# A gelu moved in ScalarE's order, thirteen split matmuls and new offsets of the 320-column operands, in a gated spectral mixer with a GeGLU branch

## The chip, the cores and the metric

The kernel runs on one core of one Trainium2 chip. The metric is the time of one execution on the device in microseconds (us); the median of several executions is compared.

## The reference, cut to what matters

```python
def _A_ref(x, w1, b1, w2, b2):
    z = rfft2(x, axes=(1, 2)).reshape(B, H, Wf, 4, 160)          # x is (2, 1, 4096, 640)
    hr = relu(zr @ w1[0] - zi @ w1[1] + b1[0]); hi = relu(zi @ w1[0] + zr @ w1[1] + b1[1])
    or_ = hr @ w2[0] - hi @ w2[1] + b2[0];      oi_ = hi @ w2[0] + hr @ w2[1] + b2[1]
    # both shrunk towards zero by 0.01
    return irfft2(or_ + 1j * oi_)
def _B_ref(x, w_gate, w_up, w_down):
    return (gelu(x @ w_gate) * (x @ w_up)) @ w_down              # 640 -> 1728 -> 640
g = sigmoid((x * gate_w).sum(-1, keepdims=True))
return g * _A_ref(...) + (1 - g) * _B_ref(...)
```

The relu, the blocks of 160 columns and the tanh form of gelu are written short here.

## The kernel before, in words

Every product is made of float32r operands in a high and a low part: a weight (wh, wl) and a moving operand (xh, xl) give three matmuls wh xh, wh xl and wl xh into one PSUM bank (`prod`, `run`, `mm3`). ScalarE makes the high part (`high`, L283), VectorE or GpSimd the low part (`low`, L286). The work has three stages, all of them on one core and issued in an order written out by hand.

**Stage 1, to about 1405 us: gate and up products.** The 8192 tokens are taken 512 at a time in 48 token groups (`keys`, counted by `i`): three rounds over the sixteen groups of tokens, with four, four and six pairs of weight tiles `t`. One group runs `quad` for each of its pairs, j = 0, 1, 2, ... (the first group runs `plain`). `quad` is Strassen's scheme with seven products instead of eight (g1, s3, s2, g2, s1, s4, u2), each a `run` of six or nine matmuls of 256 columns into half a bank. It is in two parts: the first four products are made at once, the last three (half5, half3, half4) are kept in `Q` and made in between the next quad's products. So the order of TensorE around the change is: half5 of the old quad (s1 into its bank X), g1 of the new quad into a new X, s3 into C, half3 of the old quad (s4 into the old X), s2 into the new X on top of g1, half4 of the old quad (u2), g2 into A.

Each bank must be read before TensorE goes on in it. ScalarE copies X after g1 (tile p, `copy`, L492), after s2 (u2) and after s1 (u4); a matmul that goes on in X waits for that copy. VectorE adds A to p1 (L516, L534 and the like for the others), ScalarE takes the gelu of p1 in place (`gelu`, L493), later the gelu of X after s4 into h, and VectorE multiplies (L536, L537). In the kernel before, the gelu of p1 stands in half5, right behind the copy of u4 and so ahead of the new quad's copy of p.

Between the products stand seven hooks per quad (`hook(0)` to `hook(6)`). They run what `spread` put into `slots`: splits of the next group's tokens (`x_prep`), preparation of weights (`w_prep`, `wd_pre`), and the 64 steps of the first transform (`a_load`, `a_split`, `a_gate`, `a_step`; `steps_a` names the group and the place of each). Each engine takes its instructions in the order in which they are issued; loads and stores of the SP queue too.

**Stage 2, to about 1842 us: the spectral branch.** Sixteen chunks of frequencies, each with four steps (64 in all, S = 64; the order of the last ones is shuffled). A chunk needs four tiles sc (`sc_load`, L746), a product `rest` whose result zz is stored to DRAM, and `zl_load`, which reads it back in another layout (L777, L779). `lead` says how many steps earlier than the others the last chunk does that. `main_z` (matmuls of 128 columns in plain float32, f and sc, L754), `mlp1`, `mlp2` (320 columns, wm with h, wl with hl), `y_split` (tile ys) and `inv1` (ys with i1) follow. `fin` lists what of the last stage is loaded in which step: `wl(part, j, ...)` loads the down weights wx that were prepared in stage 1 (`wd_load`, L1054).

**Stage 3: down projection and last transform.** 32 rounds of `down`, each of 144 matmuls of 320 columns, tile wx moving and tile ho as weights (L469), with `inv2` in between (s2s moving, v as weights, twelve matmuls).

**Where the tiles start.** Tiles come from pools: small (2560 bytes per partition each), big (5376), still (1024), mid (4096), tiny (1024). As the program lays them out, big, still and small tiles start at a multiple of 256 bytes, and mid tiles 192 bytes past one, because of the unused tile "gap" of 192 bytes. `off` shifts a view inside its tile by so many words of 4 bytes. 320 columns are 1280 bytes, five times 256, so all operands of a tile keep its place modulo 256.

Of the kernel before, what the change touches and what calls it, by code (L numbers as in the profile page):

```python
# [11 lines left out]
F32R = mybir.dt.float32r  # L12
# [200 lines left out]
def spectral_mix_kernel(ctx: ExitStack, tc: tile.TileContext, a):  # L213
# [29 lines left out]
    def big(shape, dt=F32, name="big", off=0):  # L243
        return view(pool[1].tile([P, 1344], dt, name=name, tag="big", bufs=17), shape, off)
# [4 lines left out]
    def mid(shape, dt=F32, name="mid", off=0):  # L249
        return view(pool[4].tile([P, 1024], dt, name=name, tag="mid", bufs=13), shape, off)  # L250
# [209 lines left out]
    def prod(ws, x):  # L460

        ops = []
        for (wh, wl), (xh, xl) in zip(ws, x):
            ops += [(wh, xh), (wh, xl), (wl, xh)]
        return ops

    def run(dst, ops, first=True):
        for i, (l, r) in enumerate(ops):
            nc.tensor.matmul(dst, l, r, start=first and i == 0, stop=i == len(ops) - 1, skip_group_check=True)  # L469
# [14 lines left out]

    Q = []

    def quad(key, t, hook):

        o, w = XO[key], WG[t]
        half = lambda: bank()[:, :256]  # L490
        T = lambda n: tiny([P, 256], name=n)
        copy = lambda d, s_: nc.scalar.activation(d, s_, AF.Copy)  # L492
        gelu = lambda d, s_: nc.scalar.activation(d, s_, AF.Gelu_apprx_tanh)  # L493
        old = Q.pop() if Q else [lambda: None] * 3

        old[0]()
        hook(0)
        X = half()
        run(X, prod(w["g1"], x_of(o, "b11", ("k4", 0))))
        p1 = T("p1")  # L500
        copy(p1, X)
        hook(1)
        C = half()
        run(C, prod(w["s3"], x_of(o, "t3", ("k4", 1))))
        hook(2)
        old[1]()
        hook(3)
        run(X, prod(w["s2"], x_of(o, "t2", "t5")), first=False)
        u2 = T("u2")
        copy(u2, X)  # L510
        hook(4)
        old[2]()
        hook(5)
        A = half()
        run(A, prod(w["g2"], x_of(o, "b21")))
        nc.vector.tensor_add(p1, A, p1)  # L516
        hook(6)
        v = {}

        def half5():  # L520
            run(X, prod(w["s1"], x_of(o, "t1", "t5")), first=False)
            u4 = v["u4"] = T("u4")
            copy(u4, X)
            gelu(p1, p1)
            nc.vector.tensor_add(u4, C, u4)

        def half3():
            run(X, prod(w["s4"], x_of(o, "b22")), first=False)
            h = v["h"] = small([P, 512], name="h")
            gelu(h[:, 256:], X)  # L530

        def half4():
            run(C, prod(w["u2"], x_of(o, "t4")), first=False)
            nc.vector.tensor_add(u2, C, u2)  # L534
            h = v["h"]
            nc.vector.tensor_mul(h[:, 256:], h[:, 256:], v["u4"])  # L536
            nc.vector.tensor_mul(h[:, :256], u2, p1)  # L537
            h_store(key[1], t, h)
        Q.append([half5, half3, half4])
# [406 lines left out]
    def y_split(b, c, pb):  # L946
        for j in range(2):
            y = Y.pop((b, c, pb, j))
            t = YS[b, c, pb, j] = big([P, 2, 2, 320], F32R, name="ys")
            split(t[:, 0], t[:, 1], y.rearrange("p r n o -> p r (n o)"),  # L950
                  nc.gpsimd if j == 1 and (b, c, pb) < (1, NCH - 2, 1) else nc.vector)

# [94 lines left out]
    def wd_load(j, part):  # L1047
        d = WM.setdefault(j, {})
        kinds = {(5, 2): ((big, 4), (small, 2)), (6, 1): ((small, 2),) * 2, (6, 2): ((small, 2),) * 3}.get(
            (j, part), (((big, 4),) if part < 2 else ((mid, 3),) * 2))  # L1050
        at_, parts = 4 * part, []

        def go(t, k, n):
            ld(t.rearrange("p h d -> p (h d)").bitcast(F32), dr(wdf[j], 320 * k, [[14 * 320, P], [1, 320 * n]]))  # L1054
        for i, (kind, n) in enumerate(kinds):
            off = {} if kind is small else {"off": 16} if kind is mid else {"off": 63 if j > 4 else 0}
            t = kind([P, n, 320], F32R, name="wx", **off)
            if part < 2 or i == 0:
                go(t, at_, n)
            else:  # L1060
                later.append(lambda t=t, k=at_, n=n: go(t, k, n))
            parts += [t[:, k] for k in range(n)]
            at_ += n
        for k in range(len(parts) // 2):
            d[FORMS[2 * part + k]] = parts[2 * k], parts[2 * k + 1]
# [7 lines left out]
            S2[i].append(raw)  # L1073

    def c_split(i):
        m = [mid([P, 3, 320], F32R, name="s2s", off=15) for k in range(3)]
        raws, S2[i] = S2[i], {}
        for k in (0, 2, 1, 3):
            h, l = (m[(2 * k + e) // 3][:, (2 * k + e) % 3] for e in range(2))
            split(h, l, raws[k // 2][:, 320 * (k % 2):320 * (k % 2) + 320])  # L1080
            S2[i][k] = h, l
# [34 lines left out]
        d["s4"] = d.pop("s2")  # L1116

    def h_op(i, name, eng=nc.vector):
        t = big([P, 5, 2, P], F32R, name="ho", off=1)
        uh, ul = (still([P, 2, P], F32R, name="ho") for k in range(2))  # L1120
        src, six = HR[i].pop(name) if name in ("s1", "s3", "s4", "a22") else HR[i][name]
        split(t[:, :, 0], t[:, :, 1], src, eng)
        if name == "a22":
            high(uh[:, 0], six[:, 0])
            high(ul[:64, 1], six[:64, 1])
            high(uh[64:, 1], six[:64, 1])
            low(ul[:, 0], six[:, 0], uh[:, 0], eng)
            low(uh[:64, 1], six[:64, 1], ul[:64, 1], eng)
        elif name in HALF:
            high(uh, six)  # L1130
            low(ul[:, 0], six[:, 0], uh[:, 0], eng)
            low(uh[64:, 1], six[:64, 1], uh[:64, 1], eng)
        else:
            high(uh, six)
            low(ul, six, uh, eng)
        HO[i, name] = [(t[:, j, 0], t[:, j, 1]) for j in range(5)] + [(uh[:, j], ul[:, j]) for j in range(2)]
# [92 lines left out]
    at(46, 2, gates, 1)  # L1229

    def i1_load():
        I1.append(big([P, 5, 2, P], F32R, name="i1", off=1))
        nc.gpsimd.dma_start(I1[0], a["i1"])
    last = len(keys) - 1
    at(last - 1, 1, i1_load)
# [32 lines left out]
    def spread(i, s, fs):  # L1268

        for k, f in enumerate(fs):  # L1270
# [1 line left out]
            while j < last and q >= points(j):  # L1272
                j, q = j + 1, q - points(j)
            slots.setdefault((j, q), []).append(f)
    steps_a = [(i, j) for i in (*range(2, 16, 3), *range(17, 31), *range(33, 46)) for j in range(1 if i < 17 else 2 if i < 33 else 3)][:64]

    def back(i, s, f):
        if s < 0:
# [38 lines left out]
    for i, key in enumerate(keys):  # L1317
        gr, tp = key
        nxt = keys[i + 1] if i < last else None
        quads = [t for t in groups[gr] if t < NPAIR]  # L1320
        nq = len(quads)
        if nxt:
            if not i:
                x_raw(nxt)
            z = 7 * (nq - 1)
            for k, s in enumerate((5, 8, 11, 14, 16, 18, z + 1, z + 4, z + 6) if gr < 2 else
                                  (6, 9, 13, 17, 21, z + 1, z + 2, z + 3, z + 3, z + 5)):
                if k < 9 or nxt[0] == 2:
                    f0, f1, f2_ = x_prep(nxt, k)
                    spread(i, s - 1, [f0])  # L1330
                    spread(i, s + 1, [f1, f2_])
            if gr < 2 and nxt[0] == 2:
                spread(i, z + 7, x_prep(nxt, 9))
        for j, t in enumerate(quads):
            def hook(k):
                for f in slots.get((i, 7 * j + k), ()):
                    f()
            (quad if i else plain)(key, t, hook)
            if gr == 2 and j == 1:
                mixed(key)  # L1340
            if i % 16 == 15:
                WG.pop(t)
            if 0 < i + 1 < last and j == nq - 1:
                x_raw(keys[i + 2])
            n = len(late)
            for f, *args in todo.get((i, j), []):
                f(*args)
            new = late[n:]
            del late[n:]
            flush()  # L1350
            late.extend(new)
        for q in range(7 * nq, 7 * nq + 14) if i == last else ():
            for f in slots.get((i, q), ()):
                f()
        XO.pop(key)
# [9 lines left out]
    todo = {}  # L1365
    for ch in range(1, 2 * NCH):
        b, c = chunks[ch]
        lead = 1 if ch == 2 * NCH - 1 else 0
        if ch > 1:
            at(4 * ch - 4 - lead, 0, sc_load, b, c)  # L1370
        at(4 * ch - 3 - lead, 1, rest, b, c)
        at(4 * ch - 2 - lead, 1, zl_load, b, c)
# [7 lines left out]
    def events(i, j):  # L1380
        for f, *args in todo.get((i, j), []):
# [3 lines left out]
           S - 13: wl(0, 1),  # L1385
           S - 12: [*wl(2, 6), (wd_later,)],
           S - 11: [*wl(2, 0), (wd_later,)],
           S - 10: wl(1, 6),
           S - 8: [(v_load, 0), *wl(2, 1), (wd_later,)],
           S - 6: wl(0, 2),  # L1390
           S - 5: wl(0, 3, 4, 5),
# [91 lines left out]
```

## Time and profile before

| | |
|---|---|
| median of 3 runs | 2579.09 us (2576.34 to 2587.95) |
| the profiled execution's own time | 2581.51 us |
| its span, first to last instruction | 2579.8 us |
| mean granted clock of TensorE | 0.997 |
| TensorE busy | 2555.5 us (99%), 20340 matmuls |
| VectorE, ScalarE, GpSimd busy | 2020.8 us (78%), 1504.9 us (58%), 381.4 us (15%) |

How to read it: PE is TensorE's matmuls, PEld its weight loads, DVE is VectorE, ACT ScalarE, POOL GpSimd, SP the queue that issues most DMAs. A row of a group has the line, the engine, the operation, what is written and read, the shapes and the count, then busy time in us and the mean duration of one in ns, then the idle time ahead of them and what ended most of it. Matmuls overlap: one lasts about 0.28 us (256 columns) or 0.31 us (320 columns) from its start to its end, while the next starts much sooner. In a timeline row stand the start, the length of the merged instructions, the engine and the line, and in brackets how long the engine was idle before and for what. A row of the waits has who waited for whom, the total in us, how often and the longest.

### The profile page before, as it was taken

Reading aid. Unit: us, or ns where it says so; the run is one execution under the profiler, and the core shown is the slowest. Engines: PE = TensorE matmul, PEld = TensorE weight load, DVE = VectorE, ACT = ScalarE, POOL = GpSimd, SP = SyncE. Lnnn points to the kernel's source line nnn. Section 1 sums busy time; section 2 is a strip of 40 time slices with the busy share of each in tenths; the row PEclk is TensorE's granted clock in tenths of the full one; section 3 lists DMA queues with packets and bytes.
Section 4 is the critical chain, followed back from the end, with each engine's and each line's share of the span. In section 5 each row is a group of like instructions: output and inputs, shape, how many; then the busy total and the mean of one; then the engine's idle time right before and its main releaser. Section 6 shows DMA issues by size and latency. Waiting matters only on the chain.

```text
span 2579.8 us, 54180 instructions
## 1 busy us (share of the span) xinstructions
PE 2555.5 (99%) x20340; PEld 2548.2 (99%) x20340; DVE 2020.8 (78%) x4179; ACT 1504.9 (58%) x3540; POOL 381.4 (15%) x382
## 2 busy tenths in 40 slices
PE   9999999999999999999999999999999999999999
PEld 9999999999999999999999999999999999999999
DVE  7767677777778777787547886887899899889997
ACT  5555555666665566666445886787644444444443
POOL 0000000000000000000002111111233333333332
PEclk9999999999999999999999998999999999999999
DMA  6555556676676677777566543547844443444432
GB/s 226 184 195 195 186 192 224 216 228 219 210 226 220 202 225 235 241 243 228 186 217 189 156 144 121 166 142 244 287 152 149 154 153 134 134 149 154 154 134 92
DMA packets 337562, 483.81 MB, mean 188 GB/s; under 512 B 25676, under 2 KB 207948, under 8 KB 337300
## 3 DMA queue, kind: packets, MB, share of 16 engines
q1 hardware_dynamic: 321748, 438.80, 52.6%
q0 software_dynamic: 15552, 41.56, 4.8%
q8 instruction: 160, 2.62, 0.4%
q14 instruction: 102, 0.84, 0.1%
HBM read 300.62 MB, written 179.64 MB: 186 GB/s over the span
## 4 chain that ended last, share of the span: by engine, by line
PE 95%; DMA 2%; DVE 2%; ACT 1%; issue 0%; SPq 0%; DVEq 0%; ACTq 0%
PE bank L469 76%; PE bank L302 13%; PE bank L754 3%; PE bank L613 1%; PE bank L810 1%; PE bank L811 1%; DMA zl<-zl 0%; DMA xraw<-in_xT_dram 0%; DMA zl<-zz 0%; PE bank L813 0%; DMA wx<-wdf 0%; DMA sc<-scr 0%; ACT xs L283 0%; DVE wl L710 0%; DVE as L615 0%
## 5 line engine op out<-in xcount | busy, mean ns | idle before, releaser
L469 PE MATMUL bank<-xo,w 128*128 128x256 f32 x11736 | 1371.7, 278 | 15.2 <-ACT p L492 7.8
L469 PEld LDWEIGHTS bank<-xo,w 128*128 128x128 f32 x11736 | 1359.5, 188 | 19.7 <-ACT p L492 10.5
L469 PE MATMUL bank<-wx,ho 128*128 128x320 f32 x4608 | 682.5, 309 | 0.0
L469 PEld LDWEIGHTS bank<-wx,ho 128*128 128x128 f32 x4608 | 678.5, 188 | 0.0
L492 ACT ACTIVATE u<-bank 128x256 f32<-128x256 f32 x408 | 156.6, 384 | 291.2 <-PE bank L469 287.3
L283 ACT ACTIVATE ho<-hraw 128x640 fp32r<-128x640 f32 (+3 forms) x384 | 179.4, 518 | 150.0 <-PE bank L469 149.2
L286 DVE TENSOR_TENSOR ho<-hraw,ho 128x640 fp32r<-128x640 f32 (+3 forms) x384 | 241.6, 678 | 4.1 <-ACT ho L283 3.1
L534 DVE TENSOR_TENSOR u<-bank,u 128x256 f32<-128x256 f32 x204 | 86.4, 423 | 134.8 <-PE bank L469 131.6
L286 DVE TENSOR_TENSOR xs<-xr,xs 64x640 fp32r<-64x640 f32 x128 | 105.0, 820 | 77.6 <-ACT xs L283 71.8
L286 DVE TENSOR_TENSOR xo<-xraw,xo 128x512 fp32r<-128x512 f32 x209 | 143.1, 685 | 21.3 <-ACT xo L283 19.7
L615 DVE TENSOR_TENSOR as<-bank,as 64x320 f32<-64x320 f32 x256 | 113.8, 483 | 28.3 <-ACT as L614 27.2
L283 ACT ACTIVATE xo<-xraw 128x512 fp32r<-128x512 f32 x209 | 129.2, 626 | 5.4 <-DMA xraw<-in_xT_dram 4.4
L302 PE MATMUL bank<-wm,h 128*128 128x320 f32 x768 | 131.6, 305 | 0.0
L493 ACT ACTIVATE h<-bank 128x256 f32<-128x256 f32 x204 | 78.0, 382 | 91.8 <-PE bank L469 88.0
L493 ACT ACTIVATE p<-p 128x256 f32<-128x256 f32 x204 | 84.5, 414 | 60.1 <-DVE p L516 59.4
L1097 POOL TENSOR_TENSOR hraw<-hraw 128x640 f32<-128x640 f32 x64 | 87.4, 1381 | 217.7 <-DMA hraw<-hD 132.8
L302 PEld LDWEIGHTS bank<-wm,h 128*128 128x128 f32 x768 | 114.5, 187 | 0.1
L286 DVE TENSOR_TENSOR s2s<-s,s2s 128x320 fp32r<-128x320 f32 x128 | 113.4, 943 | 0.5 <-ACT s2s L283 0.5
L566 POOL MEMSET h<- 64x512 f32 x16 | 8.4, 522 | 707.8 <-PE bank L469 338.1
L283 ACT ACTIVATE ho<-hs 128x640 fp32r<-128x640 f32 (+1 forms) x128 | 67.1, 572 | 70.4 <-PE bank L469 65.5
L1160 ACT ACTIVATE uu<-bank,gs 128x320 f32<-128x320 f32 x120 | 54.3, 525 | 89.4 <-PE bank L302 89.4
L614 ACT ACTIVATE as<-bank 64x320 f32<-64x320 f32 x256 | 96.8, 427 | 15.6 <-PE bank L613 12.8
(168 smaller groups left out, 3507.8 us busy)
## 6 DMA issues: line engine op xcount, KB each, us to landing
xo<-xD SPq DMA_DIRECT2D x124, 512.0 KB
xraw<-in_xT_dram SPq DMA_DIRECT2D x225, 256.0 KB
hD<-h SPq DMA_DIRECT2D x224, 256.0 KB
hraw<-hD SPq DMA_DIRECT2D x128, 320.0 KB
xD<-xo POOLq DMA_DIRECT2D x64, 512.0 KB, 4.2
xr<-in_x_dram SPq DMA_DIRECT2D x64, 320.0 KB
scr<-as SPq DMA_DIRECT2D x64, 320.0 KB
sc<-scr SPq DMA_DIRECT2D x64, 320.0 KB
```

Source lines behind the costliest of these rows:

```text
L283: nc.scalar.activation(dst, src, AF.Copy, scale=scale)
L286: eng.tensor_sub(dst, src, hi.bitcast(F32))
L302: nc.tensor.matmul(dst, l, r, start=i == 0, stop=i == len(ops) - 1)
L469: nc.tensor.matmul(dst, l, r, start=first and i == 0, stop=i == len(ops) - 1, skip_group_check=True)
L492: copy = lambda d, s_: nc.scalar.activation(d, s_, AF.Copy)
L493: gelu = lambda d, s_: nc.scalar.activation(d, s_, AF.Gelu_apprx_tanh)
L534: nc.vector.tensor_add(u2, C, u2)
L614: nc.scalar.activation(stg[hi, cs], pa[lo, :320], AF.Copy)
L615: nc.vector.tensor_add(stg[hi, cs], pa[hi, :320], stg[hi, cs])
L754: nc.tensor.matmul(pz[:, kp * P:(kp + 1) * P], SC[b, c, kp][:, o:o + P], ft, start=True, stop=True)
L1097: eng.tensor_sub(d["a21"][k], d["a11"][k], d["a21"][k])
L1160: nc.scalar.activation(uu[n2][:, cs], pe[:, :320], AF.Copy, scale=gs[:, b, 0, n2:n2 + 1])
```

## The change

It does six things.

- In `quad` the gelu of p1 moves from half5 to the head of half3. On ScalarE it then comes behind the new quad's copy of p and behind what hooks 0, 1 and 2 issue, ahead of the gelu of h.
- `quad` gets an argument `fresh`. Where it holds, the last matmul of the product g2 is written as two matmuls of 128 columns with the same weights. It holds for the second pair (j = 1) of the token groups 1, 2, 5, 9, 13, ... 45, thirteen times in all.
- The offsets: ys goes from the start of its big tile to 15 words; wx from 0 or 63 words (big) and 16 (mid) to 15 and 31; s2s (mid) from 15 to 31; ho and i1 (big) from 1 word to 0. In bytes modulo 256: ys and most wx from 0 to 60, the wx of the pairs 5 and 6 in big tiles from 252 to 60, s2s from 252 to 60, ho and i1 from 4 to 0. wx in small tiles stay at 0, v stays at 0.
- The list of the 64 steps of the first transform has none in token group 14 any more; all later ones move on by one place.
- The last chunk of stage 2 has its loads and its `rest` two steps ahead instead of one.
- The two loads of wx for pair 6, part 1, come in step S - 7 instead of S - 10.

```diff
-    def quad(key, t, hook):
+    def quad(key, t, hook, fresh):
...
         A = half()
-        run(A, prod(w["g2"], x_of(o, "b21")))
+        ops = prod(w["g2"], x_of(o, "b21"))
+        if fresh:
+            run(A, ops[:-1])
+            for q in (slice(0, P), slice(P, 256)):
+                run(A[:, q], [(ops[-1][0], ops[-1][1][:, q])], first=False)
+        else:
+            run(A, ops)
         nc.vector.tensor_add(p1, A, p1)
...
             copy(u4, X)
+            nc.vector.tensor_add(u4, C, u4)
+
+        def half3():
             gelu(p1, p1)
-            nc.vector.tensor_add(u4, C, u4)
-
-        def half3():
             run(X, prod(w["s4"], x_of(o, "b22")), first=False)
...
-            t = YS[b, c, pb, j] = big([P, 2, 2, 320], F32R, name="ys")
+            t = YS[b, c, pb, j] = big([P, 2, 2, 320], F32R, name="ys", off=15)
...
-            off = {} if kind is small else {"off": 16} if kind is mid else {"off": 63 if j > 4 else 0}
+            off = {} if kind is small else {"off": 31} if kind is mid else {"off": 15}
...
-        m = [mid([P, 3, 320], F32R, name="s2s", off=15) for k in range(3)]
+        m = [mid([P, 3, 320], F32R, name="s2s", off=31) for k in range(3)]
...
-        t = big([P, 5, 2, P], F32R, name="ho", off=1)
+        t = big([P, 5, 2, P], F32R, name="ho")
...
-        I1.append(big([P, 5, 2, P], F32R, name="i1", off=1))
+        I1.append(big([P, 5, 2, P], F32R, name="i1"))
...
-    steps_a = [(i, j) for i in (*range(2, 16, 3), *range(17, 31), *range(33, 46)) ...
+    steps_a = [(i, j) for i in (*range(2, 14, 3), *range(17, 31), *range(33, 46)) ...
...
-            (quad if i else plain)(key, t, hook)
+            if i:
+                quad(key, t, hook, j == 1 and (i % 4 == 1 or i == 2))
+            else:
+                plain(key, t, hook)
...
-        lead = 1 if ch == 2 * NCH - 1 else 0
+        lead = 2 if ch == 2 * NCH - 1 else 0
...
-           S - 10: wl(1, 6),
+           S - 7: wl(1, 6),
```

More of the change, by code (lines that the diff above doesn't have):

```diff
@@ L523, in half5 @@
             copy(u4, X)
-            gelu(p1, p1)
             nc.vector.tensor_add(u4, C, u4)
         def half3():
+            gelu(p1, p1)
             run(X, prod(w["s4"], x_of(o, "b22")), first=False)
@@ L1274, in spread @@
             slots.setdefault((j, q), []).append(f)
-    steps_a = [(i, j) for i in (*range(2, 16, 3), *range(17, 31), *range(33, 46)) for j in range(1 if i < 17 else 2 if i < 33 else 3)][:64]
+    steps_a = [(i, j) for i in (*range(2, 14, 3), *range(17, 31), *range(33, 46)) for j in range(1 if i < 17 else 2 if i < 33 else 3)][:64]
     def back(i, s, f):
```

## The prediction

> **What bounds the kernel now.** I read the page's busy times and its chain first, then the groups by shape, then who waited for whom, then the timeline around each wait, and last stretches of equal work side by side.
>
> ```profile
> span 2579.8 us, 54180 instructions
> PE 2555.5 (99%) x20340; PEld 2548.2 (99%) x20340; DVE 2020.8 (78%) x4179; ACT 1504.9 (58%) x3540; POOL 381.4 (15%) x382
> PE 95%; DMA 2%; DVE 2%; ACT 1%; issue 0%; SPq 0%; DVEq 0%; ACTq 0%
> L469 PE MATMUL bank<-xo,w 128*128 128x256 f32 x11736 | 1371.7, 278 | 15.2 <-ACT p L492 7.8 <-ACT xo L283 5.1 <-ACT u L492 1.4
> L469 PE MATMUL bank<-wx,ho 128*128 128x320 f32 x4608 | 682.5, 309 | 0.0
> ```
>
> TensorE holds 95% of the chain and is never far from its next matmul, so only three things can be won: the idle time in front of its matmuls, the pace at which it takes one after another, and the number of them. VectorE at 78% and ScalarE at 58% matter only where one of them keeps TensorE waiting.
>
> ```profile
> PEld bank L469 <- ACT p L492: 10.5, 11, 2.8
> PEld bank L469 <- ACT xo L283: 5.1, 1, 5.1
> PEld bank L469 <- ACT u L492: 2.2, 4, 1.0
> ACT p L493 <- DVE p L516: 59.4, 80, 3.1
> ```
>
> The 5.1 us are the start of the program. The rest of the first stage's idle time is ScalarE's copy of the gate's first product (p, L492), 10.5 us in 11 waits. What holds that copy up is seen in one of them:
>
> ```profile
> 781.48 0.38 ACT L492 ACTIVATE u<-bank 128x256 f32<-128x256 f32 x1 [0.22 <-PE bank L469]
> 783.55 0.42 DVE L516 TENSOR_TENSOR p<-bank,p 128x256 f32<-128x256 f32 x1
> 784.00 0.42 ACT L493 ACTIVATE p<-p 128x256 f32<-128x256 f32 x1 [2.14 <-DVE p L516]
> 784.45 0.73 ACT L283 ACTIVATE xs<-xr 64x640 fp32r<-64x640 f32 x1
> 785.20 0.42 ACT L283 ACTIVATE w<-wt 128x256 fp32r<-128x256 f32 x1
> 785.52 0.37 ACT L492 ACTIVATE p<-bank 128x256 f32<-128x256 f32 x1
> 785.94 2.27 PE L469 MATMUL bank<-xo,w 128*128 128x256 f32 x17 [1.78 <-ACT p L492]
> ```
>
> ScalarE is free at 781.86, but the next in its queue is the old group's gelu of p, which waits 2.14 us for VectorE's sum of p (behind other work in VectorE's queue). Two splits and the new group's copy of p stand behind that gelu, and TensorE, which writes the same bank next, behind the copy.
>
> **The pace.** The same 256-column matmuls run at two paces with nothing waiting and the clock at 1.00 in both (columns: stretch, length, busy us and count of PE, PEld, DVE, ACT, POOL, then the granted clock, the DMA share and GB/s):
>
> ```profile
> 42.00:72.00 30.00, 30.00 (x256) 30.00 (x256) 23.94 (x56) 17.30 (x43) 2.67 (x5) 1.00 0.59 193
> 77.00:107.00 30.00, 30.00 (x267) 30.00 (x266) 19.41 (x43) 14.94 (x37) 3.20 (x6) 1.00 0.63 210
> 700.00:780.00 80.00, 80.00 (x699) 80.00 (x698) 58.87 (x133) 50.37 (x118) 0.00 (x0) 1.00 0.70 225
> 787.00:925.00 138.00, 138.00 (x1168) 138.00 (x1167) 101.09 (x241) 80.43 (x199) 2.10 (x4) 1.00 0.69 214
> 936.00:1000.00 64.00, 64.00 (x541) 64.00 (x540) 48.10 (x107) 38.48 (x91) 1.04 (x2) 1.00 0.69 213
> 1012.00:1072.00 60.00, 60.00 (x524) 60.00 (x523) 46.03 (x103) 37.50 (x88) 1.04 (x2) 1.00 0.70 215
> ```
>
> 30 us over 267 matmuls is 112.4 ns, over 256 it is 117.2; 80/699 is 114.4 ns, 138/1168 is 118.2, 64/541 is 118.3, 60/524 is 114.5 (the later stretches hold a few 320-column matmuls). The long dear stretch starts at 785.94, right behind the wait shown above. A third view shows a dear stretch ending at matmuls of 128 columns:
>
> ```profile
> 1359.75 6.52 PE L469 MATMUL bank<-xo,w 128*128 128x256 f32 x54
> 1366.11 1.05 PE L754 MATMUL bank<-f,sc 128*128 128x128 f32 x8
> ...
> 1367.12 4.70 PE L469 MATMUL bank<-xo,w 128*128 128x256 f32 x40
> ```
>
> One matmul alone lasts about 0.28 us, so the others ahead take (6.52 - 0.28)/53 = 117.7 ns and those behind (4.70 - 0.28)/39 = 113.3 ns. A wait can thus start the dear pace, it then lasts by itself, and short matmuls end it.
>
> **The change part by part.**
>
> *Gelu of p behind the copy of p.* Nothing is added on any engine. The gelu now comes after hooks 1 and 2, some eighteen matmuls (2.0 us) later, when VectorE's sum is mostly there: the longest of the 80 waits was 3.1 us. Behind it now stand the gelu of h and the copy of u2. TensorE needs that copy only after twelve more matmuls (1.4 us), and VectorE needs the gelu only in half4. Of 10.5 us I count 10 as gone. The waits of the 80 that stay are covered by those 1.4 us; without that cover up to 59.4 us would come back (a rival below).
>
> *One step of the first transform taken from token group 14.* Each later step takes the place of the one after it, and the last third has one more; TensorE's work is the same. ScalarE and VectorE lose two splits and four evictions each in group 14, where one more wait stands:
>
> ```profile
> 377.33 1.79 PEld L469 LDWEIGHTS bank<-xo,w 128*128 128x128 f32 x15 [0.97 <-ACT u L492]
> ```
>
> I count 1 us for it. Between 0 and 2.2 (all four waits for u) is possible.
>
> *The split matmul.* It comes in 13 groups (1, 2, 5, 9, ... 45) once each. A 128-column matmul is not cheaper than a 256-column one here: in the eight at 1366.11 the others take (1.05 - 0.28)/7 = 110 ns ahead of the last. So each split adds one matmul of about 113 ns at most: 13 x 0.113 = +1.5 us. In return the dear pace lasts no longer than about four token groups. At the cheap pace the four dear stretches in the windows would have taken 256 x 112.4 = 28.8 us, 1168 x 114.4 = 133.6, 541 x 114.5 = 61.9: 1.2 + 4.4 + 2.1 = 7.7 us less. The one from 785.94 and the one after it go twice over: their wait goes, and a split would end them. I count -7.5. If the splits do nothing and the dear pace starts anyway, it is 0; from below, a dear pace in fewer places than this execution had cannot give more than about 9.
>
> *The last chunk's loads one step earlier* (and two tiles of the last stage's operands loaded later, out of their way on SP's queue):
>
> ```profile
> 1778.78 0.46 PE L754 MATMUL bank<-f,sc 128*128 128x128 f32 x2 [0.16 <-DVE y L844]
> 1779.46 0.49 PE L754 MATMUL bank<-f,sc 128*128 128x128 f32 x2 [0.22 <-DMA sc<-scr]
> 1780.24 0.49 PE L754 MATMUL bank<-f,sc 128*128 128x128 f32 x2 [0.29 <-DMA sc<-scr]
> 1781.04 1.38 PE L754 MATMUL bank<-f,sc 128*128 128x128 f32 x10 [0.30 <-DMA sc<-scr]
> 1782.17 0.60 PE L302 MATMUL bank<-zs,wm 128*128 128x256 f32 x3
> ...
> 1794.91 0.50 PE L302 MATMUL bank<-z,wm 128*128 128x256 f32 x3
> 1796.07 0.38 PE L302 MATMUL bank<-zl,wl 128*128 128x256 f32 x1 [0.66 <-DMA zl<-zl]
> 1796.95 0.39 PE L302 MATMUL bank<-zl,wl 128*128 128x256 f32 x1 [0.50 <-DMA zl<-zl]
> 1797.18 0.52 PE L302 MATMUL bank<-z,wm 128*128 128x256 f32 x3
> ```
>
> The row before 1779.46 to the one at 1782.17 is sixteen matmuls in 3.39 us where 16 x 0.11 = 1.8 would do: 1.6 lost. Then five take 2.27 where 0.57 would do: 1.7 lost. What is moved is four loads of sc, the store of zz and the five loads of zl; on SP's queue they pass two stores of is and some loads of wx, which the last stage reads only steps later. From 1782.17 to 1794.91 are two steps, so a step is about 6 us, longer than either delay, and the 3.3 us should go; buffers that come free late may keep part. I count 3, between 0 and 3.3.
>
> *The offsets.* The moved columns wx (last stage), ys and s2s now start 60 bytes past a multiple of 256, their weights ho, v and i1 at one (the few wx in small tiles stay at a multiple). Before, wx and ys mostly started at a multiple with weights 4 bytes past it, and s2s at 252 past one with weights at one. The pace by such classes:
>
> ```profile
> 2069.52 1.90 PE L302 MATMUL bank<-s2s,v 128*128 128x320 f32 x12
> 2071.25 21.33 PE L469 MATMUL bank<-wx,ho 128*128 128x320 f32 x144
> 2092.42 1.90 PE L302 MATMUL bank<-s2s,v 128*128 128x320 f32 x12
> ...
> L302 PE MATMUL bank<-wl,hl 128*128 128x320 f32 x256 | 58.2, 308 | 0.7 <-ACT is L971 0.7
> ```
>
> Starts of groups, from one to the next: s2s (2071.25 - 2069.52)/12 = 144.2 ns, wx (2092.42 - 2071.25)/144 = 147.0 ns. The wl matmuls come in 128 pairs, are placed as the change wants it (60 and 0), and take 58.2/128 - 0.308 = 0.147 us from the first to the second. So the bounds for wx are 144.2 and 147.0, and wl, the nearest by place, speaks for the upper one; but its pairs stand behind others, while s2s is a run of twelve with the same 60 bytes past a multiple of 64. I take 145.0: 4608 x 2.0 ns = -9 us. The bounds are -13 and 0; should s2s go to 147, +1. No row shows a pace above this for such operands without a wait, so I put no larger loss in the range.
>
> The Trainium skill, "TensorE: Matmul & The Clock Gate", in the step list of "Part 2: What happens when you issue a matmul", says that moving columns and weights have independent read ports and that loading weights takes no bandwidth from the running matmul. By that rule no offset could change the pace and the sum would be 2561.5; the trace speaks against it, with 144.2 beside 147.0 ns for the same 320 columns at clock 1.00.
>
> *The sum.* The profiled execution took 2581.5 us (span 2579.8), 2.4 above the median 2579.1 of runs that spread over 11.6. -10 - 1 + 1.5 - 7.5 - 3 - 9 = -29: 2552.5, rounded to 2552.
>
> **The rivals.**
>
> *The offsets do nothing.* The wx pace stays near 147 as wl has it: 2581.5 - 20 = 2561.5, still faster by 0.7%. For it: wl. Against: s2s.
>
> *The waits go, the dear pace stays, the offsets do nothing.* The splits cost their 1.5 and end nothing, and some start of the program brings the dear pace on: 2581.5 - 10 - 1 - 3 + 1.5 = 2569. Against it: the cheap pace behind 1366.11.
>
> *Gelu's wait moves to the copy of u2.* If VectorE's sum of p is late by more than the 2.0 us of the move plus the 1.4 us that TensorE leaves for u2, it stops TensorE again. With all 59.4 us handed on it would be 2612, slower by 1.3%; it decides the sign from about 29 us, and slower by over 0.5% from 42 us. Against it: 3.1 us is the longest of the 80 waits, so hardly one passes 3.4.
>
> *The gelu move does not free TensorE*, because hook 0's splits, which stay ahead of the copy, are what is late: half of the 10 stays and the dear pace with it, 2565 with the offsets.
>
> **How the numbers follow.** A measurement of this kernel tells about 0.5% (13 us) from no change, that is 2566. Forecast 0.54; offsets nothing 0.25; dear pace stays and offsets nothing 0.10; gelu move half in vain 0.08; u2 waits 0.03. Faster takes the first, most of the second and half of the fourth: 0.81. Same: 0.16; slower: 0.03. The low end is all bounds at their best, 2581.5 - 10.5 - 2.2 - 9 - 3.3 - 13 + 1.5 = 2545, and 4 of the runs' scatter below that, 2541. The high end takes in the 2569 case: 2570.
>
> **What would show it.** Right: no wait of TensorE for the copy of p; 1168 matmuls of the stretch behind 787 in some 134 us; 144 wx matmuls in 20.9 us instead of 21.17; no sc or zl wait near 1780. Wrong: 21.2 us or more for the 144; waits for u in place of p; dear stretches running past a split.

## The result and the profile after

The changed kernel takes 2562.64 us in the median of 4 runs (2561.78 to 2563.66), against 2578.08 us (2576.34 to 2587.95, 4 runs) for the kernel before beside it: a ratio of 0.9932, 95% interval 0.9907 to 0.9958. Six more runs in a later series gave 2561.26 us (2558.59 to 2563.24), ratio 0.9915 [0.9898, 0.9933]. A ratio leaves disturbed runs out (beside the later kernels, one run of the kernel before took 3376.76 us at a granted clock of 0.70), so it is not always the quotient of the two medians. The changed kernel is faster by 0.7 to 0.9%, where 1.1% was forecast. The profiled execution took 2563.2 us, 18.3 less than the one before; the forecast was 29 less.

The page of the changed kernel and its groups by shape, to be read against the first rows of the prediction:

```profile
span 2561.4 us, 54289 instructions
PE 2542.9 (99%) x20353; PEld 2537.2 (99%) x20353; DVE 2019.6 (79%) x4179; ACT 1501.9 (59%) x3540; POOL 379.4 (15%) x382
PE 97%; DVE 1%; DMA 1%; ACT 1%; issue 0%; POOL 0%; SPq 0%; DVEq 0%; ACTq 0%
L469 PE MATMUL bank<-xo,w 128*128 128x256 f32 x11723 | 1368.4, 277 | 10.1 <-ACT xo L283 5.1 <-ACT u L492 2.8 <-ACT p L492 1.8
L469 PE MATMUL bank<-wx,ho 128*128 128x320 f32 x4608 | 673.2, 306 | 0.1
```

TensorE now holds 97% of the chain instead of 95%. The wx group has lost 9.3 us; the idle time ahead of the gate's matmuls has gone from 15.2 to 10.1 us, of which 5.1 are the start of the program. Who waited, from the view of waits of the changed kernel:

```profile
PEld bank L469 <- ACT u L492: 3.5, 4, 1.8
PEld bank L469 <- ACT p L492: 2.4, 3, 1.4
PEld bank L469 <- DVE p L522: 0.8, 4, 0.2
```

The waits for p fell from 10.5 us in 11 to 2.4 in 3, but those for u grew from 2.2 to 3.5. The pace in stretches (columns as in the prediction):

```profile
787.00:916.00 129.00, 129.00 (x1131) 129.00 (x1130) 95.91 (x228) 77.60 (x192) 1.56 (x3) 1.00 0.72 223
918.00:991.00 73.00, 73.00 (x616) 73.00 (x615) 55.42 (x122) 45.48 (x106) 1.04 (x2) 1.00 0.75 236
1207.00:1296.00 89.00, 89.00 (x754) 88.80 (x753) 51.23 (x118) 43.85 (x107) 2.56 (x5) 1.00 0.68 217
700.00:780.00 80.00, 80.00 (x699) 80.00 (x699) 60.11 (x134) 50.58 (x119) 0.00 (x0) 1.00 0.68 220
```

From 787 on it is 129/1131 = 114.1 ns, where it was 118.2. But the next stretch is dear (73/616 = 118.5), and so is one from 1207 to 1296 (118.0), where the kernel before ran cheaply. The dear pace moved more than it shrank. The offsets, in the timeline:

```profile
2058.67 1.89 PE L302 MATMUL bank<-s2s,v 128*128 128x320 f32 x12
2060.40 20.99 PE L469 MATMUL bank<-wx,ho 128*128 128x320 f32 x144
2081.23 1.89 PE L302 MATMUL bank<-s2s,v 128*128 128x320 f32 x12
```

(2081.23 - 2060.40)/144 = 144.7 ns against 147.0.

The starts of all matmuls in the two traces split the 18.3 us. Of a distance between the starts of two 256-column matmuls, the part above 113.3 ns is counted as dear pace where the distance is 115 to 121 ns, and as a wait where it is longer.

| term | forecast | measured |
|---|---|---|
| waits in stage 1 (gelu move and the step taken from group 14) | -10 - 1 | 19.4 to 12.8: -6.6 |
| 13 splits: 60 + 109 + 172 ns for the two halves and the matmul behind, instead of 2 x 113.3 | +1.5 | +1.5 |
| dear pace | -7.5 | 10.96 to 7.91: -3.05 |
| stage 2 (last chunk's loads) | -3 | 437.5 to 436.6: -0.9 |
| stage 3 (offsets) | -9 | 732.7 to 723.4: -9.3 |
| sum | -29 | -18.3 |

One part of stage 3 is not the change's doing. In the changed kernel's trace the clock that TensorE was granted stood at 0.50 from 1832.5 to 1835.9 us:

```profile
1833.20:1835.90 2.70, 2.70 (x12) 2.70 (x12) 1.85 (x4) 1.45 (x5) 0.00 (x0) 0.50 0.77 300
```

There the first ten wx matmuls start 266 or 267 ns apart instead of 144.6, which costs 1.3 us. Without that, stage 3 would be 10.6 us shorter than before.

### The profile page after: what moved, and what is told of

It reads as the page before. It is cut to its first block, busy times and chain, and to the rows that moved or that the text cites. A ratio compares the mean times of both kernels' runs of the same rounds, so it can differ in the third digit from the quotient of the medians.

```text
span 2561.4 us, 54289 instructions
## 1 busy us (share of the span) xinstructions
PE 2542.9 (99%) x20353; PEld 2537.2 (99%) x20353; DVE 2019.6 (79%) x4179; ACT 1501.9 (59%) x3540; POOL 379.4 (15%) x382
## 4 chain that ended last, share of the span: by engine, by line
PE 97%; DVE 1%; DMA 1%; ACT 1%; issue 0%; POOL 0%; SPq 0%; DVEq 0%; ACTq 0%
PE bank L469 77%; PE bank L302 14%; PE bank L760 3%; PE bank L619 1%; PE bank L817 1%; PE bank L816 1%; PE bank L819 0%; DMA raw<-in_w1m_dram 0%; DMA sc<-scr 0%; DMA rl<-in_w1l_dram 0%; DVE ho L286 0%; DMA wraw<-in_wgu_dram 0%; DVE wl L716 0%; PE bank L884 0%; DVE wm L672 0%
## 5 line engine op out<-in xcount | busy, mean ns | idle before, releaser
L469 PE MATMUL bank<-xo,w 128*128 128x256 f32 x11749 | 1368.4, 277 | 10.1 <-ACT xo L283 5.1
L469 PE MATMUL bank<-wx,ho 128*128 128x320 f32 x4608 | 673.2, 306 | 0.1
L469 PEld LDWEIGHTS bank<-wx,ho 128*128 128x128 f32 x4608 | 669.2, 188 | 0.3 <-DVE ho L286 0.3
L283 ACT ACTIVATE ho<-hraw 128x640 fp32r<-128x640 f32 (+3 forms) x384 | 179.3, 517 | 147.3 <-PE bank L469 146.5
L621 DVE TENSOR_TENSOR as<-bank,as 64x320 f32<-64x320 f32 x256 | 113.8, 483 | 35.3 <-ACT as L620 33.6
L492 ACT ACTIVATE p<-bank 128x256 f32<-128x256 f32 x204 | 78.0, 382 | 70.1 <-PE bank L469 65.7
```

Source lines behind the costliest of these rows:

```text
L283: nc.scalar.activation(dst, src, AF.Copy, scale=scale)
L621: nc.vector.tensor_add(stg[hi, cs], pa[hi, :320], stg[hi, cs])
```

## The experiments

Theory at the start: the terms above add up, each from its own part, and the dear pace is what differs from run to run. Rivals: the gelu move does little by itself; the offsets matter through something else than the place of the moved columns; the splits do nothing. The first four kernels have 35 runs of the kernel before beside them (median 2580.02 us); the targeted splits, the first kernel with xo moved and the repeat have 10 (2586.89), and the last kernel has 8 (2579.66).

### The gelu move alone, on the kernel before

```diff
             copy(u4, X)
-            gelu(p1, p1)
             nc.vector.tensor_add(u4, C, u4)
         def half3():
+            gelu(p1, p1)
```

> The kernel before with the gelu of p moved and nothing else. My theory: the waits for the copy of p go from 10.5 us to 2 to 3, some of it comes back as waits for the copy of u, and fewer dear stretches start; the first stage, 1399.7 us from its first to its last matmul before, becomes 8 to 12 us shorter, the other stages stay. Rival (what the move wins is lost again to waits for u2 and to the end of the stage): the first stage is shorter by less than 4 us.

Measured: 2572.04 us, ratio 0.9968 [0.9951, 0.9984]. Stage 1 is 9.3 us shorter in its profile, but 8.0 of that is pace (the dear pace costs 2.99 us there instead of 10.96), and the waits fell by 1.7 us only, from 19.4 to 17.8. Two things in the 17.8 are not the move's. The start of the program, to 30 us, has 1.1 us more of waits than before, and in the last token group the granted clock stood at 0.50 for 3.4 us, which counts as about 1.4 us of wait:

```profile
1388.20:1391.20 3.00, 2.81 (x13) 2.81 (x14) 1.54 (x1) 1.09 (x4) 1.94 (x4) 0.50 0.90 314
```

Between 30 and 1360 us, where neither counts, the waits are 10.1 us in the kernel before and 6.5 here. Token group 14 shows what stayed. TensorE in this kernel, then ScalarE in it, then TensorE in the kernel before and in the changed one:

```profile
372.86 1.31 PE L469 MATMUL bank<-xo,w 128*128 128x256 f32 x9 [0.17 <-ACT p L492]
374.99 1.63 PE L469 MATMUL bank<-xo,w 128*128 128x256 f32 x12 [0.82 <-DVE u L524]
378.17 2.08 PE L469 MATMUL bank<-xo,w 128*128 128x256 f32 x16 [1.55 <-ACT u L492]
```

```profile
377.43 0.42 ACT L283 ACTIVATE xo<-xd 128x256 fp32r<-128x256 f32 x1 [1.19 <-DVE xd L434]
377.75 0.37 ACT L492 ACTIVATE u<-bank 128x256 f32<-128x256 f32 x1
```

```profile
373.82 2.74 PE L469 MATMUL bank<-xo,w 128*128 128x256 f32 x21 [1.98 <-ACT p L492]
```

```profile
370.83 5.40 PE L469 MATMUL bank<-xo,w 128*128 128x256 f32 x45
```

Before, the wait for p (1.98) was the large one. With the gelu moved it is 0.17, but 0.82 comes for VectorE's u and 1.55 for the copy of u2, which on ScalarE stands behind a split that waits for VectorE's xd. VectorE was late all along; the gelu was only the first to show it. Only with the step of the first transform taken out of this group as well is there no wait left (45 matmuls in one piece).

### The splits alone, on the kernel before

```diff
-        run(A, prod(w["g2"], x_of(o, "b21")))
+        ops = prod(w["g2"], x_of(o, "b21"))
+        if fresh:
+            run(A, ops[:-1])
+            for q in (slice(0, P), slice(P, 256)):
+                run(A[:, q], [(ops[-1][0], ops[-1][1][:, q])], first=False)
+        else:
+            run(A, ops)
```

`fresh` holds in the same thirteen places as in the change.

> The kernel before with the thirteen split matmuls and nothing else. My theory: each split costs about 0.13 us (1.7 in all) and ends a dear stretch; the stretch from 786 us, which ran to 926, ends at the split near 871, so the pace's extra time goes from 11 us to 6 to 8 and the first stage is 1 to 4 us shorter. Rival (a split does nothing to the pace): the first stage is 1.7 us longer and the dear stretches run past the splits.

Measured: 2578.81 us, ratio 0.9990 [0.9972, 1.0007]: no change that could be told. All waits for p are there; in its profile the wait at 784 us was followed by the cheap pace, so the dear pace cost 2.6 us, and the stretch that the split near 871 us was expected to end did not come. The one dear stretch that met a split, at 46 us, ended there.

### The offsets alone, on the kernel before

```diff
-            off = {} if kind is small else {"off": 16} if kind is mid else {"off": 63 if j > 4 else 0}
+            off = {} if kind is small else {"off": 31} if kind is mid else {"off": 15}
```

with the matching lines for ys, s2s, ho and i1.

> The kernel before with the offsets changed and nothing else. My theory: the last stage is 9 to 11 us shorter (144 wx matmuls in 20.8 us instead of 21.17), the other stages stay within 1 us, so the time is 2568 to 2570 where before has 2578. Rival (part of the last stage's gain in the full change came from somewhere else, or is given back by waits at its start): less than 7 us.

Measured: 2567.35 us, ratio 0.9959 [0.9940, 0.9978]; 144.6 ns per wx matmul and a last stage of 721.8 us, 10.9 less than before. Stage 1 is untouched (11.2 us of dear pace, all waits for p). The offsets work alone and are worth what the pace says: 4608 x (147.0 - 144.6) ns = 11 us. Of the 1.6 us that the changed kernel's last stage took longer, 1.3 lie in its first round (23.69 us there, 22.40 here), where its clock was halved, as shown above.

### The changed kernel without the splits

```diff
-        ops = prod(w["g2"], x_of(o, "b21"))
-        if fresh:
-            run(A, ops[:-1])
-            for q in (slice(0, P), slice(P, 256)):
-                run(A[:, q], [(ops[-1][0], ops[-1][1][:, q])], first=False)
-        else:
-            run(A, ops)
+        run(A, prod(w["g2"], x_of(o, "b21")))
```

> The changed kernel without the split matmuls. My theory: 1.7 us less work, but a dear stretch, once begun, runs on: where the splits at 45 and 1296 us ended one, it lasts until a wait ends it, 30 to 55 us longer each, which costs 1 to 3.5 us; the time is between 1.5 us shorter and 2 us longer than the changed kernel's 2562.6. Rival (splits are needed all the time): the dear pace holds for most of the first stage and it is over 10 us longer.

Measured: 2560.52 us (2553.56 to 2582.99, 12 runs), ratio 0.9925 [0.9903, 0.9946]. Its profile has the longest dear stretch of all, next to the same stretch of the changed kernel:

```profile
510.00:790.00 280.00, 280.00 (x2359) 280.00 (x2359) 201.39 (x448) 168.66 (x395) 1.07 (x2) 1.00 0.67 215
800.00:925.00 125.00, 125.00 (x1098) 125.00 (x1097) 93.25 (x220) 74.84 (x185) 1.57 (x3) 1.00 0.71 225
```

```profile
510.00:780.00 270.00, 270.00 (x2353) 270.00 (x2352) 200.59 (x447) 167.28 (x393) 1.07 (x2) 1.00 0.69 221
```

280/2359 = 118.7 ns until a wait at 793 ended it, and 125/1098 = 113.8 behind; 114.7 in the changed kernel. Without splits the dear pace lasted 290 us here; the longest dear stretch in any trace with the thirteen splits is 92 us. In the median the two kernels can't be told apart. The ten runs with splits lie between 2558.6 and 2563.7, the twelve without between 2553.6 and 2583.0. That the splits keep the runs together is not shown by this: the six runs of the repeat and the twelve without splits come from different chips, and the twelve runs with the splits alone spread over 11.6 us (2574.6 to 2586.2).

### The repeat of the changed kernel, and splits where the waits are

```diff
-                quad(key, t, hook, j == 1 and (i % 4 == 1 or i == 2))
+                quad(key, t, hook, (i, j) in ((1, 1), (14, 2), (19, 2), (30, 2)) or j == 4 and i in (34, 36, 38, 40, 42))
```

The two long stretches that were dear after the change begin at small waits for VectorE's p. The one ahead of the second, in TensorE's weight loads:

```profile
1207.29 1.83 PEld L469 LDWEIGHTS bank<-xo,w 128*128 128x128 f32 x15 [0.20 <-DVE p L522]
```

> The changed kernel with its split matmuls at nine places instead of thirteen: behind the start (token group 1), behind the three copies that ended late in the profile of the changed kernel (token groups 14, 19, 30) and behind the small waits for VectorE's p in token groups 34 to 42. If a wait starts the dear pace and a split ends it, the stretches 917 to 991 and 1207 to 1297 us shrink to a few us each: the extra time of the dear pace goes from 7.9 us to 2 or 3, and with four splits fewer (0.5 us) the time falls by 5 to 6 us, to about 2557. If the dear pace comes and goes by chance, the extra stays between 3 and 14 us and the time within 3 us of the changed kernel's.

> The changed kernel once more, so that the two others have it on their own chip: 2562.6 within 4 us. If the dear pace is set by where waits happen to end, the 13 splits should keep its runs close together, as the first four were (2561.8 to 2563.7); if these four were luck, they spread over 10 us or more like those of the kernel without splits.

Measured: the repeat 2561.26 us, as above, with its six runs within 4.7 us; the targeted splits 2562.1 us (2556.42 to 2569.73), ratio 0.9924 [0.9899, 0.9949]. In the profile with targeted splits the dear pace began at three of these waits and was ended by the split behind each (at 920, 992 and 1064 us):

```profile
917.00:991.00 74.00, 74.00 (x642) 73.80 (x642) 58.25 (x129) 47.82 (x114) 1.04 (x2) 1.00 0.77 244
```

74/642 = 115.3 ns against 118.5 in the changed kernel's, and the dear pace costs 3.35 us. The mechanism was as expected. The numbers of the rival, chance, would fit as well (3 to 14 us of dear pace, a time within 3 us of the changed kernel's); what speaks against it is that these stretches end at the splits. The time came only in part. The profiled execution took 2557.39 us, the 2557 that was expected, and three of the six runs lie between 2556.4 and 2558.2; the other three lie between 2566.0 and 2569.7, and no trace shows what they lost. In the median there is no gain, and the scatter is larger than with the regular splits. In its repeat the changed kernel itself had only 4.33 us of dear pace, so there was less to win than the 7.91 us of its first profile.

In the eight traces with splits and with xo at its old place, a split met the dear pace 18 times and ended it 18 times. Splits are not the only thing that ends it: the changed kernel's stretch from 917 us ended at 991, 16 us ahead of the next split, behind two matmuls of the first transform.

### Where the moved columns start

Four kernels start from the changed kernel and change only the start of wx, ys and s2s past a multiple of 256 bytes: 252, 0, 32 and 4 instead of 60 (the offsets in words, big then mid, are 63 and 15, 0 and 16, 8 and 24, 1 and 17). The first is shown; the lines for ys and s2s match.

```diff
-            off = {} if kind is small else {"off": 31} if kind is mid else {"off": 15}
+            off = {} if kind is small else {"off": 15} if kind is mid else {"off": 63}
```

> The changed kernel, but wx, ys and s2s start 252 bytes past a multiple of 256 instead of 60; weights as in the changed kernel, at a multiple. Theory A (what counts is where the moved columns start within 64 bytes; 252 and 60 are both 60 past a multiple of 64): the 144 wx matmuls keep the changed kernel's 144.6 ns each, about 20.85 us from the first to the next group. Theory B (the distance of 60 to the weights counts, by 256): back to about 147.0 ns, 21.17 us.

> The changed kernel with wx, ys and s2s at a multiple of 256, as their weights are. Theory A (start within 64 bytes): 147.0 ns per wx matmul, and ys and s2s go to about 147 too, although before they were at 144.2 (s2s). Theory C (what made wx dear before was that its weights lay 4 bytes past a multiple; multiples on both sides are good): 144.6 ns. Time by A about 2563 + 4608 x 0.0024 = 2574 us, by C about 2563.

> The changed kernel with wx, ys and s2s 32 bytes past a multiple of 256. Theory D (any start off a multiple of 64 avoids the dear pace): 144.6 ns per wx matmul. Theory E (60 past a multiple of 64 alone does): about 147.0 ns. I lean to E, since 60 leaves one element in front of the next 64 bytes, but no row shows a start at 32 so far.

> The changed kernel with wx, ys and s2s 4 bytes past a multiple of 256, so that the last element instead of the first lies by itself. Theory D (any start off a multiple of 64): 144.6 ns per wx matmul. Theory E (60 past alone): about 147.0 ns.

The wx group of the four, in that order:

```profile
L469 PE MATMUL bank<-wx,ho 128*128 128x320 f32 x4608 | 671.8, 306 | 0.6 <-DVE ho L286 0.6
```

```profile
L469 PE MATMUL bank<-wx,ho 128*128 128x320 f32 x4608 | 681.6, 309 | 0.4 <-DVE ho L286 0.3
```

```profile
L469 PE MATMUL bank<-wx,ho 128*128 128x320 f32 x4608 | 680.4, 309 | 0.3 <-DVE ho L286 0.3
```

```profile
L469 PE MATMUL bank<-wx,ho 128*128 128x320 f32 x4608 | 702.0, 315 | 0.0
```

By the starts that is 144.5, 146.7, 146.5 and 151.2 ns from one wx matmul to the next, beside 144.6 at 60 (in each mean are the few wx in small tiles, which stay at a multiple); one run each took 2563.1, 2570.0, 2566.1 and 2598.8 us (the kernel before 2577.3, also one run); a single time is weak evidence, the 4608 distances in each trace are not. So 60 and 252, both 60 past a multiple of 64, are alike; a multiple and 32 past one are 2 ns dearer; 4 past one is 6.6 ns dearer, 30 us in 4608. Theory A (the start within 64 bytes counts) holds and theory B (the distance to the weights by 256) falls. Theory E (60 alone is good) holds among the four places tried, theory D (any start off a multiple of 64) falls, and so does theory C: with columns and weights both at a multiple the pace is 146.7 ns and not 144.6. The weights' 4 bytes in the kernel before had a small part in its 147.0. Told apart by their place in the round of 144, its pairs 0 to 4 (columns at a multiple, weights 4 bytes past one) take 147.4 ns and its pairs 5 and 6 (columns mostly at 252, weights in tiles that start at a multiple) 145.6; beside the 146.7 the weights' part is some 0.7 ns in pairs 0 to 4. What other places of the weights would do is not shown; they stayed at a multiple in the four kernels here.

### The same offset for the 256-column operands

The natural next step is to put the gate's own columns (xo) at 60 too. In the first of two kernels the weights' tiles moved as well, so that they start at any multiple of 64; in the second they stay.

```diff
-                m = mid([P, 2, 512], F32R, name="xo")
+                m = mid([P, 2, 512], F32R, name="xo", off=15)
```

The same stands in both places where such a tile is made. In both kernels the tiles of the mid pool are also made 16 elements longer.

> The changed kernel with the gate's own moved columns (xo, but for the 1224 matmuls on its smallest tile) 60 bytes past a multiple of 64 too; its tiles of that pool are 16 elements longer and those of the largest pool 16 shorter, so that they stay at multiples of 64. Theory P (the start within 64 bytes sets the pace of any moved columns): the 256-column matmuls run below 113.3 ns, by the share of the 320-column ones (144.6 beside 146.7, 1.4%) 1.6 ns over some 10500 matmuls, about 17 us, and the dear pace may be gone with it, 8 more: 2540 to 2547. Theory Q (at 256 columns the two paces have another cause): 113.3 and 117.8 ns as before, 2562 within 4.

> The gate's moved columns (xo) 60 bytes past a multiple of 64, as in the run that came out at 2606 us, but with the tiles of the largest pool at their old places, so that every weight stays at a multiple of 256; in that run the weights had gone to 64, 128 and 192 past one as well. If the start of xo made the dear pace the rule there: 117 to 118 ns for nearly all 256-column matmuls again, about 2605 us. If the weights' places did: 113.3 ns with a few dear stretches, 2562 within 5.

Measured: 2605.99 us, ratio 1.0088 [1.0072, 1.0105], and 2602.68 us, ratio 1.0078 [1.0053, 1.0102]: 40 us or more above the changed kernel. One stretch of each, in that order:

```profile
700.00:780.00 80.00, 80.00 (x678) 80.00 (x677) 56.82 (x127) 47.42 (x112) 0.00 (x0) 1.00 0.64 208
```

```profile
700.00:780.00 80.00, 80.00 (x678) 80.00 (x677) 56.92 (x127) 47.35 (x112) 0.00 (x0) 1.00 0.64 208
```

678 matmuls where the changed kernel has 699: 118.0 against 114.4 ns. The dear pace is the rule from the start to the end of stage 1 (10820 of the 11723 matmuls lie between 115 and 121 ns in the second), and none of the 13 splits in either kernel ends it. Theories P and Q both fall: the start of the columns does set the pace at 256 columns, but there 60 is the bad place. The weights' places are not needed for it, since both runs show it. The longer tiles of the mid pool, which both kernels have too, were not tried alone.

## Why the prediction was right or wrong, step by step

The time came out in the stated range and on the right side, 10 us above the forecast. It lies almost at the 2561.5 us of the rival "the offsets do nothing", and that is chance: the offsets gave all that was forecast, while the waits came out 4.4 us short, the dear pace 4.5 and the loads 2.1. The total alone would have spoken for the wrong rival.

**The gelu move (-10) and the step from group 14 (-1).** The sum was 4.4 us short and its division wrong. That TensorE no longer waits for the copy of p held up to 1360 us; the 2.4 us that are left lie in the last groups. The step that failed is "Of 10.5 us I count 10 as gone". It took for granted that nothing else on ScalarE is late. Between 30 and 1360 us the waits are 10.1 us before, 6.5 with the gelu moved, 2.8 in the kernel without splits and 3.8 in the changed one (restarts behind splits left out). So the move took 3.6 off there, and up to 3.7 more came with the rest of the change. The three waits of group 14 shown above make 2.5 of these, where the step taken from that group was priced at 1. What else of the change has a part in them was not separated, and the step alone was not run. What was late next was named as a rival, the copy of u2, and it came: not from the 59.4 us of the gelu's waits, but through splits that wait for VectorE. At 783 us, TensorE and then ScalarE of the changed kernel:

```profile
783.63 1.30 PE L469 MATMUL bank<-xo,w 128*128 128x256 f32 x9 [0.65 <-ACT u L492]
```

```profile
782.89 0.42 ACT L283 ACTIVATE xo<-xd 128x256 fp32r<-128x256 f32 x1 [1.64 <-DVE xd L434]
783.21 0.36 ACT L492 ACTIVATE u<-bank 128x256 f32<-128x256 f32 x1
```

Of the 1.78 us there, 0.65 stayed. And in the last token group 4.9 us of waits stayed of some 5.3 (ScalarE and the weight loads):

```profile
1379.07 0.74 ACT L283 ACTIVATE bh<-rs 66x640 fp32r<-66x640 f32 x1 [1.80 <-DVE rs L694]
...
1380.34 0.36 ACT L492 ACTIVATE p<-bank 128x256 f32<-128x256 f32 x1
...
1380.75 1.11 PEld L469 LDWEIGHTS bank<-xo,w 128*128 128x128 f32 x9 [1.38 <-ACT p L492]
...
1388.64 0.42 ACT L283 ACTIVATE zs<-zt 128x256 fp32r<-128x256 f32 x1 [3.06 <-DVE zt L770]
...
1388.96 0.36 ACT L492 ACTIVATE u<-bank 128x256 f32<-128x256 f32 x1
...
1389.38 0.75 PEld L469 LDWEIGHTS bank<-xo,w 128*128 128x128 f32 x6 [1.84 <-ACT u L492]
```

Here the copies stand behind the preparation of the next stage's weights (bh) and of zs, which wait for VectorE (rs, zt). The gelu has no part in it.

**The splits (+1.5)** cost what was said: 60 + 109 + 172 = 341 ns for 227, 13 times. The size is right by luck. It rested on plain float32 matmuls of 128 columns that start 110 ns apart; the first half of a float32r split lets the next matmul start after 57 to 61 ns, and what makes up for it is the matmul behind the two, which takes 170 to 172 ns to the next start instead of 113.

**The dear pace (-7.5, came out at -3).** That a wait can start it, that it lasts by itself, and that a split ends it were right, the last on evidence that did not carry it: the short matmuls at 1366 us were plain float32, and groups of that kind begin the dear pace as often (last section). The 1168 matmuls behind 787 would take 133.2 us at the measured 114.1 ns, where 134 was said. The step that failed is "a split would end them" as a price: it counted the dear stretches of the one execution shown (the text says four, the sum has three) and left new ones out. New ones came, at waits of 0.2 us for VectorE's p (0.8 us in 4) that the kernel before has too:

```profile
PEld bank L469 <- DVE p L516: 0.6, 3, 0.2
```

By the starts of the matmuls, the four traces without splits and with xo at its old place (before, gelu, offsets, no splits) have 11.0, 3.0, 11.2 and 14.2 us of dear pace; the seven with the thirteen splits have 7.9 (after), 2.6 (splits alone), 10.7, 7.9, 4.4 and 10.2 (starts at 252, 0, 32 and 4) and 4.3 (repeat). So this term changes by several us from execution to execution, and one profile can't price it.

**The loads (-3, came out at -0.9).** One wait of the six near 1780 is left. TensorE of the changed kernel:

```profile
1763.76 0.83 PE L760 MATMUL bank<-f,sc 128*128 128x128 f32 x6
1764.97 1.38 PE L760 MATMUL bank<-f,sc 128*128 128x128 f32 x10 [0.38 <-DMA sc<-scr]
1766.11 0.60 PE L302 MATMUL bank<-zs,wm 128*128 128x256 f32 x3
```

Sixteen matmuls take 2.35 us where 1.8 would do, so 0.55 of the 3.3 us is left. Half of what was won is lost again ahead of the last stage. The weight loads after the change:

```profile
1821.27 0.73 PEld L302 LDWEIGHTS bank<-wm,h 128*128 128x128 f32 x5 [0.36 <-DVE h L795]
1822.97 0.30 PEld L302 LDWEIGHTS bank<-wl,hl 128*128 128x128 f32 x2 [0.96 <-ACT is L977]
...
1826.80 2.03 PEld L302 LDWEIGHTS bank<-s2s,v 128*128 128x128 f32 x14 [0.92 <-DVE s2s L286]
1830.05 0.19 PEld L302 LDWEIGHTS bank<-ys,i 128*128 128x128 f32 x1 [1.22 <-ACT ys L283]
1831.19 1.78 PEld L302 LDWEIGHTS bank<-ys,i 128*128 128x128 f32 x11 [0.96 <-DVE ys L286]
```

That is 4.4 us; before it was 3.1 (0.97 for ACT is, 0.50 for DVE s2s, 0.63 for ACT ys and 0.97 for DVE ys). The prediction looked for the price of the move only up to the next two steps. Stage 2 takes 434.8 to 439.1 us in the four traces without this part (mean 437.0) and 433.7 to 437.2 in the five with it whose columns start at 60 or 252 (435.5), so even the sign of the rest rests on a difference within the scatter. Most of that scatter is the clock: it stood at 0.50 for 10.2 to 17.1 us of stage 2, differently in each trace (13.7 before, 14.3 after). An estimate that counts half of that time as lost leaves 429.7 to 430.7 us without this part and 428.5 to 430.4 with it, so 0.6 in the mean and still not clear of the scatter. The cause of the longer waits at the end was not tried.

**The offsets (-9, came out at -9.3)** were the best of the terms: s2s was the right guide, not wl, and the rival that they do nothing (a quarter of the chance) is excluded by the run with the offsets alone. That the size fits to 0.3 us is chance: the pace gave 2.4 ns instead of the 2.0 taken, 11 us, and the halved clock in the first round took 1.3 of it back. The 147 ns for wl, worked out from busy time, was too high; by the starts its pairs take 145.9 ns before. Why that is still above the 144.6 of wx at the same place is not shown. The reason given (60 past a multiple of 64 as s2s has it) holds for 320 columns. The rule of the Trainium skill named in the prediction ("TensorE: Matmul & The Clock Gate", Part 2) says that loading weights takes no bandwidth from the running matmul, and the prediction read from it that no offset could change the pace. That reading fails: at one granted clock of 1.00 the runs show 144.5 to 151.2 ns for the same matmul, by the start of its moved columns alone. The rule itself is about the loading of weights, and no run here tests it.

## What to carry to other kernels

When one engine is late, moving the instruction that waits for it only shows the next one that does: list everything in the queue behind it that depends on the same late engine, and price the move at what is left after that. A stall seen at one place is a fair price only for that place; an effect that comes and goes between executions needs several traces. Where operands lie in memory can cost as much as a reordering of engines, and the good place must be measured for each width of matmul: 60 bytes past a multiple won 11 us at 320 columns and lost 40 at 256.

## What the runs showed of the hardware that was not expected

- The pace of float32r matmuls depends on where their moved columns start, and not the same way for all widths: at 320 columns 144.6 ns at 60 bytes past a multiple of 64, 146.6 at 0 and 32, 151.2 at 4; at 256 columns 113.3 ns at a multiple (117.8 in dear stretches) and 117 to 118 nearly always at 60.
- The dear stretches go with the restart. Over the twelve traces with xo at its old place, take the first gate matmul behind a wait or behind matmuls of the first transform, and look at the pace from the seventh matmul on. Where the second starts 226 or 227 ns after the first, the dear pace followed in 28 of 30 cases; at 223 or 224 ns in 1 of 43; at 225 in 6 of 14, and at 221 or 222 in 18 of 82. Behind the short float32 matmuls (f, sc) the distance is 200 or 201 ns with the dear pace behind it 13 times in 13, or 202 to 206 with the cheap one 11 times in 11. The prediction took the one such group that it showed (1366.11) as an end of the dear pace; these groups begin it as often. This is an order in the traces, found afterwards; no run set the restart on purpose.
- Two matmuls of 128 columns in place of one of 256 cost 114 ns more and ended the dear pace 18 times in 18, but not once in the two kernels where the operands' start made it, 13 splits each.
- The granted clock falls to 0.50 for 3.4 or 10.2 us at a time, and not only where TensorE pauses: from 1580 to 1590 us the changed kernel has 10.00 us of matmuls in 10.00, at 0.50. Every trace has such a stretch of 10.2 us within some 40 us of there, and up to three of 3.4 us elsewhere ahead of its end. If half of that time is lost, an estimate, two traces differ by up to 5 us from this alone.
